# Pooled attention and a GELU MLP on one core: the loads of the fourth group placed behind the transposes of the softmax weights

## The chip, the cores and the metric

The kernel runs on one core of a Trainium2 chip. The metric is device time in microseconds (us), taken as the median of several runs. The kernel before took 294.56 us (three runs, 293.27 to 294.96). The profiled execution of it has a span of 291.9 us. All times inside the kernel are counted from the start of that span.

## What is computed

Eight batches of attention come first. Keys and values are averaged over blocks of eight rows, so that 576 queries meet 72 pooled keys. Then every token passes an MLP with a tanh GELU. Shapes: q, k and v are 8 x 8 heads x 576 x 64, in float32; the MLP goes from 512 to 2048 and back to 512, for 4608 tokens.

```python
k_p = k.reshape(B, H, Sp, pool, D).mean(axis=3)        # pool = 8, Sp = 72
v_p = v.reshape(B, H, Sp, pool, D).mean(axis=3)
scores = scale * np.matmul(q, k_p.transpose(0, 1, 3, 2))
attn = np.exp(scores - scores.max(-1, keepdims=True))
attn = attn / (attn.sum(-1, keepdims=True) + 1e-09)
x = np.matmul(attn, v_p)                               # then heads side by side: 4608 x 512
h = x @ w_in
g = 0.5 * h * (1.0 + np.tanh(c * (h + 0.044715 * h * h * h)))
out = g @ w_out
```

## The kernel before

The tokens are taken in nine groups. Groups 0 to 7 are the first 512 queries of each batch; the remainder R holds the last 64 queries of all eight batches. The order is 0, 1, ..., 6, R, 7, and **step n** is the MLP of the n-th group in it. The kernel is a software pipeline. While step n runs its MLP on TensorE, the attention of the next group (n+1) is worked out in between, and the inputs of the group after that (n+2) are loaded. So step 1 runs the MLP of group 1, the attention of group 2 and the loads of group 3.

Instructions are placed by hand. `at(hooks, slot, f, ...)` says ahead of which matmul of the step's MLP a piece of other work is put into the programs of its engines. Slots 0 to 63 lie in the first half of the MLP (64 matmuls with w_in, "hidden"), slots 64 to 175 in the second (seven products of 16 matmuls each). A slot fixes the order of the instructions on each engine, not a time: an instruction starts when it is at the head of its engine's program and what it waits for has come.

All DMAs are issued by SyncE, one after the other: loads, stores, and the three kinds of transposes that the DMA engines do. `kTd` is the transposed pooled K, `qT` the transposed queries, `eT` the transposed softmax weights, in four parts j = 0 to 3.

```python
if kv:
    t0 = 22 if n_ == 1 else 12
    at(hooks, t0, pool, b, 0, 5)             # VectorE: sums K (and the first half block of V) over 8 rows
    at(hooks, t0, dup_k, b, 0, 5)
    at(hooks, t0, kT_tile, b, None)
    at(hooks, t0, k_transpose_dma, b)        # SyncE: kTd
    t1 = t0 + (16 if n_ == 1 else 24)
    at(hooks, t1, pool, b, 5, 9)             # VectorE: the rest of V
    at(hooks, t1, spread_v, b, nc.gpsimd)
    at(hooks, 56, k_spread, b, [nc.vector, nc.vector])
for j in range(4):
    sj = 64 + ([4, 4, 30, 34] if n == R else [4, 7, 28, 36])[j]
    at(hooks, sj, scores, n, j)              # TensorE
    at(hooks, sj, exps, n, j)                # ScalarE
    ...
    nj = 64 + [17, 33, 40, 50][j]
    at(hooks, nj, norm, n, j, nc.gpsimd if j == 1 else nc.vector)   # writes eb
    at(hooks, nj, e_transpose_dma, n, j)     # SyncE: eT, part j
...
at(hooks, 64 + 92, values_part, n, 0, [nc.scalar, nc.vector])       # TensorE: needs eT parts 0 and 1
...
if n_ > 1:
    at(hooks, 4, values_part, g, 1, [nc.scalar, nc.vector])         # parts 2 and 3, in the next step
```

`pool` sums blocks c0 to c1 of one tile that holds K and V. Blocks 0 to 3 are K; block 4 is half K and half V; blocks 5 to 8 are V. So `pool(b, 0, 5)` waits for three loads, and `pool(b, 5, 9)` for the fourth:

```python
def load_kv(n):
    if n != B - 1:
        b = B - 1 if n == R else n
        kv_tile(b)
        load_main(b, "k", 0, 4, nc.sync)     # 1 MB
        load_half(b, "k", nc.sync)           # 128 KB
        load_half(b, "v", nc.sync)           # 128 KB
        load_main(b, "v", 0, 4, nc.sync)     # 1 MB
```

In the second half of the MLP, the sums of activations (`g_sums`, VectorE) and the copy of the first product out of its PSUM bank (`x_copy`, VectorE) come ahead of the product called 6, which reads the sums and writes that bank again:

```python
for n, (prod, acc, fresh) in enumerate([(1, xs, 1), (2, y, 1), (6, xs, 0), (5, z, 1), (7, xs, 0), (3, z, 0), (4, xs, 0)]):
    ...  # 16 matmuls of product `prod` into bank `acc`
    if prod == 1:
        x_copy(nc.vector, k2)
```

After the norms, `cast_gated` (GpSimd) turns the queries of the group after the next into bf16, and `q_transpose_dma` transposes them at slot 164, for the scores of the next step.

Of the kernel before, what the change touches and what calls it, by code (L numbers as in the profile page):

```python
# [19 lines left out]
def kernel(  # L20
# [21 lines left out]
    nc = tc.nc  # L42
# [10 lines left out]
    R = B  # L53
# [622 lines left out]
    def at(hooks, s, f, *a):  # L676
        hooks.setdefault(s, []).append(lambda: f(*a))
# [6 lines left out]
    hooks = {}  # L684
# [42 lines left out]
    for n_, g in enumerate(seq):  # L727
        if n_ == 0:
            continue
        hooks = {}  # L730
        if n_ == 1:
            for i in range(1, 4):
                at(hooks, i, w_sums, i, 0, NP, nc.vector)
            at(hooks, 36, g_sums, 0, 4)
        else:
            at(hooks, 20, g_sums, 0, 2)
            at(hooks, 36, g_sums, 2, 4)
        at(hooks, 57, g_sums, 4, 6)
        at(hooks, 65, g_sums, 6, 8)
        if n_ + 1 < len(seq):  # L740
            n = seq[n_ + 1]
            b = B - 1 if n == R else n
            kv = n != B - 1
            if n_ == 1:
                for j in range(4):
                    at(hooks, 28 + 4 * j, cast_q, n, j, j + 1, nc.scalar)
                at(hooks, 41, qT_tile, n)
                at(hooks, 41, q_transpose_dma, n)
            if kv:
                t0 = 22 if n_ == 1 else 12  # L750
                at(hooks, t0, pool, b, 0, 5)
                at(hooks, t0, dup_k, b, 0, 5)
                at(hooks, t0, kT_tile, b, None)
                at(hooks, t0, k_transpose_dma, b)
                t1 = t0 + (16 if n_ == 1 else 24)
                at(hooks, t1, pool, b, 5, 9)
# [4 lines that stand above are left out]
                at(hooks, sj, scores, n, j)  # L761
                at(hooks, sj, exps, n, j)
                if j == 0:
                    at(hooks, 64 + 17, eT_tile, n)
                nj = 64 + [17, 33, 40, 50][j]
                at(hooks, nj, norm, n, j, nc.gpsimd if j == 1 else nc.vector)
                at(hooks, nj, e_transpose_dma, n, j)
            at(hooks, 64 + 66, nc.scalar.preload_act_table_set, GELU_SET)
            at(hooks, 64 + 92, xT_tile, n)
            at(hooks, 64 + 92, values_part, n, 0, [nc.scalar, nc.vector])  # L770
        if n_ > 1:
            at(hooks, 4, values_part, g, 1, [nc.scalar, nc.vector])
        if n_ + 2 < len(seq):
            n2 = seq[n_ + 2]
            if n2 != R:
                at(hooks, 57, q_tile, n2)
                at(hooks, 57, load_q, n2, 0, 4, nc.sync)
            at(hooks, 64 + 52, cast_gated, n2)
            at(hooks, 64 + 100, qT_tile, n2)
            at(hooks, 64 + 100, q_transpose_dma, n2)  # L780
            at(hooks, 44 if n_ == 1 else 28, load_kv, n2)
        if n_ == 1:
            at(hooks, 58, q_tile, R)
        if 1 <= n_ <= 4:
            at(hooks, 58, load_q, R, n_ - 1, n_, nc.sync)
        mlp(g, hooks, n_ + 1 == len(seq), n_ > 1)


# [28 lines left out]
```

The softmax here doesn't subtract the row's maximum and nothing guards it: scores larger than these inputs give would overflow.

## Time and profile before

The page of the profile lists each engine's busy time as a share of the span.

| | busy us | share of the span |
|---|---|---|
| TensorE matmuls (PE) | 277.1 | 95% |
| TensorE weight loads (PEld), beside them | 198.2 | 68% |
| VectorE (DVE) | 206.7 | 71% |
| ScalarE (ACT) | 166.8 | 57% |
| GpSimd (POOL) | 63.7 | 22% |
| DMA queue of SyncE, share of 16 engines | | 71.9% |

A matmul counts as busy from start to end, so the busy share says little on its own; the idle stretches, and what ends them, say more. The profile cuts the span into 40 slices of 7.3 us each, and gives each engine's busy share in tenths for each slice, with the clock that TensorE was granted. The waits name, for an engine, the instruction that sat idle and what released it. In the DMA queue's timeline a start is when SyncE began to issue the transfer, the duration is the issuing, and the time to landing is counted from the start.

### The profile page before, as it was taken

To read this page: it belongs to the slowest core of one execution; us is meant where nothing else is said; L and a number is where in the kernel's file an instruction comes from. 1 tells how busy PE (TensorE), PEld (TensorE's weight loads), DVE (VectorE), ACT (ScalarE), POOL (GpSimd) and SP (SyncE) were. 2 spreads that over 40 slices of the span, in tenths; PEclk is the share of its full clock that TensorE was granted. 3 is DMA by queue.
4 is the path that set the end of the run, shared out by engine and by line. 5 is a ranking of instruction groups with operands and counts; after the bars stand their busy time and mean duration, and the time that the engine had idled before them with its cause. 6 is when DMAs were issued, how large, how long until landed. Compare 5 with 4: busy or idle time off the path is not lost.

```text
span 291.9 us, 5584 instructions
## 1 busy us (share of the span) xinstructions
PE 277.1 (95%) x2193; PEld 198.2 (68%) x2203; DVE 206.7 (71%) x379; ACT 166.8 (57%) x262; POOL 63.7 (22%) x97
## 2 busy tenths in 40 slices
PE   7799999999669999999999999999999999999994
PEld 3578753447547498649865986598658965985583
DVE  5891879899617896789588958994899445944531
ACT  1586574786306663666467547754675467546510
POOL 4575343012120312031203120312031200100000
PEclk9999999999979999999999999999999999999999
DMA  7999999999948894899779957915731560144003
GB/s 232 353 386 342 378 384 189 324 273 268 279 89 219 268 261 94 217 266 261 111 196 315 213 124 186 310 37 137 184 129 36 130 144 2 37 99 101 1 2 145
DMA packets 71419, 56.41 MB, mean 193 GB/s; under 512 B 45664, under 2 KB 55392, under 8 KB 71392
## 3 DMA queue, kind: packets, MB, share of 16 engines
q1 hardware_dynamic: 71392, 56.04, 71.9%
q8 instruction: 17, 0.28, 0.4%
q14 instruction: 10, 0.08, 0.1%
HBM read 36.70 MB, written 9.44 MB: 158 GB/s over the span
## 4 chain that ended last, share of the span: by engine, by line
PE 79%; DMA 11%; SPq 4%; DVE 4%; issue 1%; POOL 0%
PE mm L485 31%; PE mm L380 28%; PE mm L391 8%; DMA w_out_s<-in_moe_w_out_dram 5%; PE xo L348 4%; DMA stage<-in_moe_w_in_dram 3%; PE x L485 2%; PE sc L229 2%; SPq L555 2%; DMA eT<-eb 1%; DMA qT<-q_b 1%; DVE eb L263 1%; PE mm L396 1%; DVE den L251 1%; SPq L108 1%
## 5 line engine op out<-in xcount | busy, mean ns | idle before, releaser
L380 PE MATMUL mm<-xT,w_in_b 128*128 128x512 bf16 x392 | 87.4, 379 | 0.4
L382 ACT ACTIVATE gT<-mm 128x512 bf16<-128x512 f32 x100 | 59.6, 598 | 24.9 <-PE mm L380 24.9
L380 PEld LDWEIGHTS <-w_in_b 128*128 128x128 bf16 x400 | 39.1, 98 | 45.8 <-issue 0.3
L485 PEld LDWEIGHTS <-gT 128*128 128x128 bf16 x512 | 49.4, 98 | 7.3
L169 POOL TENSOR_TENSOR vbd<-kvb,vmask 128x256 bf16<-128x256 bf16 (+2 forms) x40 | 23.6, 613 | 97.4 <-DVE kvb L149 97.3
L391 PE MATMUL mm<-xT,w_in_b 128*128 128x256 bf16 x352 | 42.2, 273 | 0.2 <-DVE xT L90 0.2
L485 PEld LDWEIGHTS <-stage 128*128 128x128 bf16 x384 | 37.4, 98 | 4.4
L391 PEld LDWEIGHTS <-w_in_b 128*128 128x128 bf16 x352 | 34.0, 98 | 4.2 <-issue 0.3
L90 DVE CAST xT<-xo 128x512 bf16<-128x512 f32 x16 | 11.1, 691 | 34.5 <-PE xo L348 29.7
L393 ACT ACTIVATE gT<-mm 128x512 bf16<-128x512 f32 x44 | 26.2, 597 | 15.4 <-PE mm L391 15.4
L485 PE MATMUL mm<-w_out_b,gT 128*128 128x256 bf16 x240 | 30.8, 273 | 0.0
L244 ACT ACTIVATE e<-sc 128x576 f32<-128x576 f32 x36 | 22.5, 650 | 11.5 <-PE sc L229 6.9
L485 PE MATMUL mm<-tw,gT 128*128 128x256 bf16 x240 | 28.8, 273 | 0.0
L88 ACT COPY osb<-mm 128x512 f32<-128x512 f32 x23 | 13.5, 587 | 26.7 <-PE mm L485 26.0
L251 DVE TENSOR_REDUCE den<-e 128x8 f32<-128x576 f32 x36 | 26.4, 734 | 2.3 <-ACT e L244 2.3
L485 PE MATMUL mm<-tw,stage 128*128 128x256 bf16 x224 | 27.9, 273 | 0.0
L147 DVE TENSOR_TENSOR kv<-kv 128x1024 f32<-128x1024 f32 (+3 forms) x19 | 21.0, 1107 | 7.9 <-DMA kv<-in_k_dram 6.1
L431 DVE TENSOR_TENSOR stage<-gT 128x512 bf16<-128x512 bf16 (+1 forms) x31 | 16.4, 528 | 12.7 <-ACT gT L382 7.4
L88 ACT CAST xT<-xo 128x512 bf16<-128x512 f32 (+1 forms) x18 | 11.3, 634 | 24.2 <-PE xo L348 16.8
L263 DVE TENSOR_TENSOR eb<-e,r 128x576 bf16<-128x576 f32 x24 | 20.4, 848 | 0.8
L432 DVE TENSOR_TENSOR gT<-gT 128x512 bf16<-128x512 bf16 (+1 forms) x31 | 14.8, 477 | 6.4 <-ACT gT L382 4.8
L263 POOL TENSOR_TENSOR eb<-e,r 128x576 bf16<-128x576 f32 x6 | 6.9, 1151 | 52.6 <-ACT e L244 46.7
(86 smaller groups left out, 301.7 us busy)
## 6 DMA issues: line engine op xcount, KB each, us to landing
kv<-in_k_dram SPq DMA_DIRECT2D x7, 1024.0 KB, 6.8
q_sb<-in_q_dram SPq DMA_DIRECT2D x7, 1024.0 KB, 11.7
out_dram<-osb SPq DMA_DIRECT2D x13, 512.0 KB, 3.0
kv<-in_v_dram SPq DMA_DIRECT2D x6, 1024.0 KB, 8.8
kv<-in_v_dram SPq DMA_DIRECT2D x4, 512.0 KB, 10.2
w_in_s<-in_moe_w_in_dram SPq DMA_DIRECT2D x4, 512.0 KB, 9.0
stage<-in_moe_w_in_dram SPq DMA_DIRECT2D x4, 512.0 KB, 11.5
w_out_s<-in_moe_w_out_dram SPq DMA_DIRECT2D x2, 1024.0 KB, 13.3
```

The lines of the kernel that those rows point to most:

```text
L88: eng.copy(out=out, in_=in_)
L147: add(out=t[:, :, 0:4, :], in0=t[:, :, 0:4, :], in1=t[:, :, 4:8, :], op=ALU.add)
L169: eng.tensor_tensor(out=vbd[p0:128, b, n0:n1, :].rearrange("p (c r) (hh d) -> p c (r hh) d", c=max(m, 1), d=D), in0=kvb[p0:128, 4 + c0:4 + ...
L244: nc.scalar.activation(out=e.rearrange("p (x h) s -> p x (h s)", x=2), in_=sc[:, :, 0:4 * Sp], func=ACT.Exp, scale=1.0 / 64.0)
L251: nc.vector.reduce_sum(out=den, in_=e, axis=AX.X)
L263: eng.tensor_tensor(out=o.rearrange("p (h s) -> p h s", s=Sp), in0=e, in1=r.unsqueeze(2).to_broadcast([128, H, Sp]), op=ALU.mult)
L380: nc.tensor.matmul(out=hp, lhsT=w_in_b[:, ko, fo * 128:(fo + 1) * 128], rhs=st[g]["xT"][:, ko, :], start=(i == 0), stop=(i == KO - 1))
L382: nc.scalar.activation(out=gT[:, fo, :], in_=hp, func=ACT.Gelu_apprx_tanh)
L391: nc.tensor.matmul(out=hp[:, f, :], lhsT=w_in_b[:, ko, (fo + f) * 128:(fo + f + 1) * 128], rhs=st[g]["xT"][:, ko, c0:c0 + 256], start=(ko ...
L393: nc.scalar.activation(out=gT[:, fo:fo + 2, c0:c0 + 256], in_=hp, func=ACT.Gelu_apprx_tanh)
L431: nc.vector.tensor_tensor(out=s3, in0=a11, in1=a21, op=ALU.subtract)
L485: nc.tensor.matmul(out=xs[p] if acc is xs else acc[:, p, :], lhsT=lt, rhs=rt, start=bool(fresh and m == 0 and (p == 0 or (last and acc is ...
```

## The change

The change moves DMA issues of SyncE, and nothing else. In the kernel before, step 1 issues at slot 44 the loads of K and V of group 3 (2.25 MB), at slots 57 and 58 the queries of group 3 (1 MB) and a part of the remainder's queries (two transfers of 128 KB, each of 512 short rows), and only then the four transposes eT of group 2. After it, step 1 issues at slot 44 only the queries of group 3, then the four transposes, then at slot 116 K and V of group 3. The four parts of the remainder's queries are loaded in steps 2 to 5 instead of 1 to 4. In step 2 the slots of the pooling are moved back, from 12 and 36 to 18 and 42.

Its purpose is that the transposes of the softmax weights of group 2 need not queue behind 3.5 MB of loads in step 1. Data, sizes and arithmetic stay the same, and so do the numbers of instructions on every engine.

```diff
@@ -747,7 +747,7 @@
             if kv:
-                t0 = 22 if n_ == 1 else 12
+                t0 = {1: 22, 2: 18}.get(n_, 12)
                 at(hooks, t0, pool, b, 0, 5)
                 at(hooks, t0, dup_k, b, 0, 5)
                 at(hooks, t0, kT_tile, b, None)
@@ -773,16 +773,17 @@
         if n_ + 2 < len(seq):
             n2 = seq[n_ + 2]
             if n2 != R:
-                at(hooks, 57, q_tile, n2)
-                at(hooks, 57, load_q, n2, 0, 4, nc.sync)
+                s2 = 44 if n_ == 1 else 57
+                at(hooks, s2, q_tile, n2)
+                at(hooks, s2, load_q, n2, 0, 4, nc.sync)
             at(hooks, 64 + 52, cast_gated, n2)
             at(hooks, 64 + 100, qT_tile, n2)
             at(hooks, 64 + 100, q_transpose_dma, n2)
-            at(hooks, 44 if n_ == 1 else 28, load_kv, n2)
+            at(hooks, 64 + 52 if n_ == 1 else 28, load_kv, n2)
         if n_ == 1:
             at(hooks, 58, q_tile, R)
-        if 1 <= n_ <= 4:
-            at(hooks, 58, load_q, R, n_ - 1, n_, nc.sync)
+        if 2 <= n_ <= 5:
+            at(hooks, 58, load_q, R, n_ - 2, n_ - 1, nc.sync)
```

## The prediction

> **What bounds the kernel now.** I read the slices first, to find where TensorE is not full; then TensorE's waits, to name what ended the gap; then busy time by step, to see what the gap costs; then the DMA queue's timeline, for the cause.
>
> ```profile
> PE   7799999999669999999999999999999999999994
> ...
> PEclk9999999999979999999999999999999999999999
> ```
>
> Each digit is 7.3 us. TensorE is full everywhere but in the first two slices, the last, and slices 11 and 12 (73 to 88 us). In the second of these the granted clock drops as well. The longest wait of TensorE stands there alone:
>
> ```profile
> PE xo L348 <- DMA eT<-eb: 5.0, 1, 5.0
> ```
>
> The columns are total us, times, longest us. L348 are the matmuls of values_part, and what they waited for is a transposed part of the softmax weights. The timeline of TensorE dates it:
>
> ```profile
> 76.50 1.47 PE L485 MATMUL mm<-w_out_b,stage 128*128 128x256 bf16 x12
> 82.99 1.86 PE L348 MATMUL xo<-eT,vbd 128*128 128x256 bf16 x8 [5.01 <-DMA eT<-eb]
> ```
>
> I took a step as running from its first matmul with w_in to that of the next, and asked for busy times of those stretches (the length comes first, then PE, PEld, DVE, ACT and POOL, the clock, the DMA share):
>
> ```profile
> 52.36:87.54 35.18, 29.67 (x201) 19.52 (x201) 25.26 (x40) 18.79 (x31) 6.32 (x9) 0.95 1.02 242
> 87.54:116.36 28.82, 28.77 (x225) 21.34 (x225) 23.20 (x42) 17.55 (x27) 6.18 (x9) 1.00 0.87 209
> 116.36:145.19 28.83, 28.78 (x226) 21.35 (x225) 23.20 (x42) 17.55 (x27) 6.18 (x9) 1.00 0.89 212
> ```
>
> Steps 2 and 3 are full of matmuls: TensorE bounds them, with 0.05 us idle. Step 1 is 6.36 us longer, though it has eight values matmuls (0.87 us) fewer, so it has about 7.2 us to give. The DMA queue's timeline says why:
>
> ```profile
> 65.41 0.59 SPq L108 DMA_DIRECT2D kv<-in_k_dram  x1
> 66.05 0.53 SPq L103 DMA_DIRECT2D kv<-in_k_dram  x1
> 66.62 0.60 SPq L101 DMA_DIRECT2D kv<-in_v_dram  x1
> 67.27 0.59 SPq L108 DMA_DIRECT2D kv<-in_v_dram  x1
> 67.90 0.62 SPq L120 DMA_DIRECT2D q_sb<-in_q_dram  x1
> 68.56 5.16 SPq L124 DMA_DIRECT2D q_r<-in_q_dram  x2
> 73.83 8.94 SPq L293 DMA_TRANSPOSE eT<-eb  x4
> ```
>
> Part 0 of the weights was ready at 72.37 us (end of its norm on VectorE), but SyncE was issuing the remainder's queries until 73.7. Once issued, part 0 took 8.0 us to land and part 1 4.4 us (issued 78.49, landed 82.9); in step 3 the same transposes take 2.6 to 2.9. The wait in step 1 is thus for 3.5 MB ahead in the queue: the last remainder load, issued 71.9, landed 9.3 us later, at 81.2, and the transposes right after it.
>
> **What the Trainium skill says.** The page "DMA: Bandwidth & Descriptors", section "Queues, rings and completion order", says that on each DMA engine the descriptors of a queue are consumed in ring order. This trace agrees: transposes ready before 75 us land just behind the loads issued before them, at 81.8 and 82.9. The same page, "Issuing engines are not separate DMA queues", says that all issuers share the same 16 engines; no run so far shows it, but it tells me that order is the only thing to gain here. The page "TensorE: Matmul & The Clock Gate", section "What's actually happening", says that an idle window of about 3.4 us halves the clock. The trace agrees: after 5.01 us idle the granted clock in 82 to 86 us is 0.56 to 0.58 and the first values matmuls take 417 ns instead of 273.
>
> **The change, part by part.**
>
> (a) The removed wait. TensorE reaches the values matmuls at 76.50 + 1.47 = 77.97. After the change only 1 MB of queries lies ahead of the transposes, issued at 65.4; at the 340 GB/s that the stretches 68 to 78 show, it is in by about 71. Part 1 is normed on GpSimd until 74.55; plus 2.6 to land is 77.2. So the wait vanishes with 0.8 us to spare: 5.0 us off.
>
> (b) The slow clock after it. From the first values matmul to the next step took 87.54 - 82.99 = 4.55 us here, 116.36 - 113.31 = 3.05 in step 2. That is another 1.5 us. Sum of (a) and (b): **6.5 us**. Step 2 would start at 77.97 + 3.05 = 81.0 instead of 87.54.
>
> (c) The moved loads. K and V of group 3 are now issued behind part 3, which is normed at 76.9 and issued from about 77.0 to 78.2. So K starts at 78.3. From the issue of K to the landing of the V half, the third transfer that the first pooling needs, it took 6.9, 8.2, 7.0 and 7.9 us in steps 2 to 5. It will land at 85.2 to 86.5, say 85.8. When would VectorE want it?
>
> ```profile
> 89.32 0.69 DVE L90 CAST xT<-xo 128x512 bf16<-128x512 f32 x1 [2.88 <-PE xo L348]
> 89.93 1.48 DVE L147 TENSOR_TENSOR kv<-kv 128x1280 f32<-128x1280 f32 x1
> ...
> 95.16 0.42 DVE L431 TENSOR_TENSOR stage<-gT 128x512 bf16<-128x512 bf16 x1 [0.16 <-ACT gT L382]
> 96.02 0.43 DVE L432 TENSOR_TENSOR gT<-gT 128x512 bf16<-128x512 bf16 x1 [0.44 <-ACT gT L382]
> ```
>
> These are VectorE's in step 2: pooling begins 2.4 us into the step, so it would want K at 81.0 + 2.4 = 83.4, **2.4 us before it is there**. Moving the pooling from slot 12 to 18 doesn't help: no other VectorE work lies between these slots, and its order of instructions is the same in both kernels. VectorE then has 0.16 + 0.44 us of waits to swallow, and none more until its last osb sum 25 us into the step: it runs about 1.8 us late through the middle of step 2.
>
> (d) What that lateness costs. Two things hang on it. First, product 6 must wait for x_copy: this ended at 105.43, and product 6 began at 106.34, so 0.9 us are free, and 1.8 late costs 0.9. Second, the transposes: pooling releases kTd, and behind it SyncE issues K and V of group 4, its queries and the remainder's, all 2.4 us later. In step 2 of before the last of these landed at 100.5 + 10.5 = 111.0, and parts 0 and 1 behind it at 111.8 and 112.6, while TensorE came for them at 113.31: 0.7 us free. Shifted by 1.8 to 2.4 us, TensorE is held 1.1 to 1.7 us in all; the 0.9 at product 6 is contained in that, not added. I take **1.5 us**. Two short waits don't reach the 3.4 us at which the clock falls.
>
> (e) The remainder's queries move from steps 1 to 4 to steps 2 to 5. Steps 2 to 4 keep one part each. Step 5 has no queries of a next group to load, so it has room; GpSimd casts them only at 198.3 us, some 11 us after that slot (slot 58 lies 58 hidden matmuls of 0.22 us and 0.9 us of values into a step that begins at 174.0). I charge nothing.
>
> Sum: 294.56 - 6.5 + 1.5 = 289.6; I round to 289.5.
>
> **The rivals.** *Full recovery*: K lands in time, or VectorE's lag is swallowed, and 6.5 us come off: 288.1. For it: K would start on a queue that holds only two transposes. Against it: K was issued on an almost empty queue in steps 2 to 5 as well and still needed 6.9 us. *A wait handed on*: step 2 becomes what step 1 was. The transposes of the queries of group 3 come behind K and V, SyncE is held in issuing them, kTd and the loads of group 4 slip 3 us or more, and TensorE waits 3 to 4 us, perhaps with the slow clock again: 291 to 293. For it: eT part 0 took 4.56 us to issue into a full queue instead of 1.2. Against it: kTd has until about 2 us ahead of the scores, and the pooling, not the queue, should end last. *Another bound at the old place*: part 1 comes from GpSimd; if it lands 1 us later than I reckon, 0.2 us of the gain go, not more.
>
> **Range and chances.** The gain is 6.5 less a hand-back between 0 and 3.5 us, most likely 1 to 2; medians of before scatter over 1.7 us. So 288.0 to 291.2 holds it 8 times in 10. Faster by over 2% means under 288.67, which needs a hand-back of 0.6 or less: 0.27. Slower by over 2% has no mechanism: 0.01.
>
> **What would show it.** Right: no wait of L348 near 78 us, no clock drop there, step 1 about 28.7 us; in step 2 a wait of VectorE's pooling (L147) for kv of about 2.4 us, and TensorE waits of 1 to 2 us at product 6 (L485, for the copy) or at L348 (for eT); step 3 again 28.8. Wrong: step 2 at 28.8 (K came in time), or at 31 and more with a clock below 1.00 (the wait was handed on), or a wait of over 0.5 us still at the first values matmuls of step 1.

## The result, and the profile after

The changed kernel takes 290.52 us (median of four runs, 289.53 to 290.72) against 294.48 us before: a ratio of 0.9869, with a 95% interval from 0.9838 to 0.9899. That is 4.0 us less. The prediction said 289.5, within 288.0 to 291.2, with a gain most likely under 2%.

The slices of the profile after, again 40 with 7.2 us each; the rows of the other engines are left out:

```profile
PE   8778999999999988999999999999999999999994
...
PEclk9999999999999999999999999999999999999999
```

The two 6s at 73 to 88 us are gone, and the clock no longer falls. Two 8s have come at 101 to 115 us, which is step 2. TensorE's waits (total us, times, longest us) name what stands there:

```profile
PE xo L348 <- DMA eT<-eb: 1.1, 1, 1.1
...
PE mm L485 <- DVE osb L90: 0.9, 1, 0.9
...
PE sc L229 <- DVE kbd L90: 0.4, 1, 0.4
```

The busy times by step, with the steps cut as before (length, then PE, PEld, DVE, ACT, POOL, clock, DMA share, GB/s), for steps 1, 2 and 3:

```profile
53.12:81.66 28.54, 28.16 (x201) 18.95 (x201) 25.04 (x40) 18.73 (x31) 6.21 (x9) 1.00 0.83 204
81.66:113.37 31.71, 29.26 (x226) 21.31 (x225) 23.21 (x42) 17.43 (x27) 6.17 (x9) 1.00 1.05 260
113.37:142.19 28.82, 28.77 (x226) 21.31 (x225) 23.20 (x42) 17.54 (x27) 6.17 (x9) 1.00 0.90 212
```

This is the whole account. Step 1 went from 35.18 to 28.54 us: **6.64 us won**. Step 2 went from 28.82 to 31.71: **2.89 us given back**. From step 3 on nothing moved. The net is 3.75 us, close to the 4.0 of the medians; the start-up was 0.76 us longer in this one profile (step 1 begins at 53.12, not 52.36), so the two spans differ by only 3.1.

The give-back begins in SyncE's DMA timeline (start, duration of the issuing):

```profile
72.93 5.99 SPq L293 DMA_TRANSPOSE eT<-eb  x4
78.98 0.57 SPq L108 DMA_DIRECT2D kv<-in_k_dram  x1
79.60 0.51 SPq L103 DMA_DIRECT2D kv<-in_k_dram  x1
80.15 0.59 SPq L101 DMA_DIRECT2D kv<-in_v_dram  x1
80.79 0.59 SPq L108 DMA_DIRECT2D kv<-in_v_dram  x1
...
82.21 8.70 SPq L220 DMA_TRANSPOSE qT<-q_b  x1
...
92.05 1.23 SPq L199 DMA_TRANSPOSE kTd<-kvb  x1
93.33 0.57 SPq L108 DMA_DIRECT2D kv<-in_k_dram  x1
```

The four transposes now land 2.6 us after each issue, as predicted. K starts at 79, and VectorE stands waiting for the third of these loads, the half block of V:

```profile
83.46 0.69 DVE L90 CAST xT<-xo 128x512 bf16<-128x512 f32 x1 [2.64 <-PE xo L348]
87.13 1.49 DVE L147 TENSOR_TENSOR kv<-kv 128x1280 f32<-128x1280 f32 x1 [2.99 <-DMA kv<-in_v_dram]
```

And TensorE pays for it at three places of step 2, with its idle time in brackets:

```profile
97.22 0.41 PE L229 MATMUL sc<-kbd,qT 128*128 128x144 bf16 x4 [0.38 <-DVE kbd L90]
...
102.11 0.60 PE L485 MATMUL mm<-tw,stage 128*128 128x256 bf16 x4 [0.93 <-DVE osb L90]
...
110.16 1.03 PE L348 MATMUL xo<-eT,vbd 128*128 128x256 bf16 x8 [1.08 <-DMA eT<-eb]
```

The three waits are 2.39 us; the remaining 0.5 us is matmuls that overlap less where TensorE has to start again (29.26 us busy against 28.77 in step 3).

### The profile page after: what moved, and what is told of

Same layout as the page of the kernel before. It is cut to its first block, busy times and chain, and to the rows that moved or that the text cites. A ratio compares the mean times of both kernels' runs of the same rounds, so it can differ in the third digit from the quotient of the medians.

```text
span 288.8 us, 5583 instructions
## 1 busy us (share of the span) xinstructions
PE 276.6 (96%) x2193; PEld 197.7 (68%) x2203; DVE 207.7 (72%) x379; ACT 166.5 (58%) x262; POOL 62.4 (22%) x97
## 3 DMA queue, kind: packets, MB, share of 16 engines
q1 hardware_dynamic: 71392, 56.04, 72.3%
## 4 chain that ended last, share of the span: by engine, by line
PE 78%; DVE 9%; DMA 8%; SPq 2%; issue 1%; POOL 1%; ACT 0%; DVEq 0%; ACTq 0%
PE mm L485 27%; PE mm L380 25%; PE mm L391 11%; PE mm L396 5%; PE xo L348 3%; DMA q_sb<-in_q_dram 3%; PE x L485 2%; DMA kv<-in_v_dram 2%; PE sc L229 2%; DMA qT<-q_b 1%; DMA eT<-eb 1%; DVE eb L263 1%; DVE kv L147 1%; SPq L108 1%; DVE w_in_b L90 1%
## 5 line engine op out<-in xcount | busy, mean ns | idle before, releaser
L90 DVE CAST xT<-xo 128x512 bf16<-128x512 f32 x16 | 11.1, 691 | 28.6 <-PE xo L348 23.7
```

## The experiments

The theory to test: eT waited in step 1 for the loads ahead of it; and of step 2's waits, the first two come from VectorE, late because the half block of V came late, the third from the DMA queue. Each run is compared with the kernel before on the same chip.

### Is it the late half block of V that costs in step 2? (K early)

```diff
 # the change, but:
-            at(hooks, 64 + 52 if n_ == 1 else 28, load_kv, n2)
+            if n_ == 1:
+                at(hooks, 44, ...)        # K and the two half blocks, 1.25 MB, right behind the queries
+                at(hooks, 64 + 52, load_main, n2, "v", 0, 4, nc.sync)
+            else:
+                at(hooks, 28, load_kv, n2)
```

> The change, but with K of group 3 and the two half blocks (1.25 MB) issued ahead of the transposes right behind the queries; only the last 1 MB of V goes behind. My theory: the first pooling of step 2 then waits for nothing, VectorE isn't late, and all three waits of TensorE in step 2 (0.38, 0.93, 1.08 us) go; 2.25 MB ahead of the transposes are in by about 74, so the wait of step 1 stays away: 288.1 us. Rival: it is the queue, not VectorE, that costs in step 2 (the queries' transposes of group 3 hold SyncE 8.7 us behind V); then the wait for eT of 1.1 us stays and this is about 289.3. Second rival: 2.25 MB ahead are too much, eT part 1 lands after 78.5, and a wait of 0.5 us or more returns in step 1.

Measured: 287.64 us, ratio 0.9762 (0.9733 to 0.9791), so clearly below the change itself. TensorE's waits from 50 us to the end, all of them:

```profile
PE xo L348 <- DMA eT<-eb: 0.5, 1, 0.5
PE sc L229 <- DMA qT<-q_b: 0.4, 1, 0.4
```

The first is in step 1 (at 78.8 us), the second was there in the kernel before as well. All three waits of step 2 are gone, and so is VectorE's for V: step 2 is 28.8 us. The second rival is right too: with 2.25 MB ahead, part 1 landed at 78.7, and 0.53 us of wait came back in step 1. It is the fastest version of this study.

### Is the third wait of step 2 the queue or VectorE? (no remainder in step 2)

```diff
-        if 2 <= n_ <= 5:
-            at(hooks, 58, load_q, R, n_ - 2, n_ - 1, nc.sync)
+        if 3 <= n_ <= 5:
+            at(hooks, 58, load_q, R, n_ - 3, n_ - 2 if n_ < 5 else 4, nc.sync)
```

> The change, but with none of the remainder's queries in step 2 (one part in steps 3 and 4, two in step 5). If the last wait of step 2 (1.08 us for eT) is the queue behind late loads, it goes, while the 0.38 for kbd and the 0.93 at product 6, which are VectorE's lateness, stay: 289.4 us. If that wait is VectorE's lateness as well (the norm of part 1 itself too late), all stays: 290.5 us. Two parts in step 5 should cost nothing, since no queries of a next group are loaded there; if they do, a wait shows in step 5.

Measured: 288.70 us, ratio 0.9808 (0.9771 to 0.9844). TensorE's waits after 50 us:

```profile
PE sc L229 <- DVE kbd L90: 0.7, 1, 0.7
PE mm L485 <- DVE osb L90: 0.6, 1, 0.6
PE sc L229 <- DMA qT<-q_b: 0.4, 1, 0.4
```

The wait for eT is gone; the two on VectorE stay and sum to 1.3 us, as with the whole change. So the third wait was the queue, filled to the end by 256 KB of short rows. Step 2 takes 30.45 us here, 1.63 more than in the kernel before: that is what VectorE's lateness costs alone. The two parts in step 5 show no wait. The time is 0.7 us lower than I expected.

### Does SyncE, held while it issues, cause the third wait? (V behind the queries' transposes)

```diff
 # the change, but K and the half blocks at slot 116, and
+                at(hooks, 64 + 101, load_main, n2, "v", 0, 4, nc.sync)     # behind q_transpose_dma at 164
```

> The whole change, but the last 1 MB of V of group 3 is issued behind the transposes of the queries of group 3, not ahead of them. K and the half blocks stay late. My theory: VectorE is as late as before (pooling waits 3 us), so the waits for kbd and at product 6 stay (1.3 us in sum); but SyncE is no longer held 8.7 us in issuing the queries' transposes, kTd goes out when K is pooled, the loads of group 4 start 1.7 us earlier, and the wait for eT in step 2 (1.08 us) falls to 0.3 or less: 289.6 us. Rival: being held is harmless and the eT wait comes from VectorE's lateness alone: 290.5 us.

Measured: 291.82 us, ratio 0.9896 (0.9861 to 0.9931): no faster than the whole change. My theory fell. TensorE in step 2, then the second pooling of VectorE:

```profile
97.92 0.41 PE L229 MATMUL sc<-kbd,qT 128*128 128x144 bf16 x4 [1.43 <-DVE kbd L90]
...
102.82 0.60 PE L485 MATMUL mm<-tw,stage 128*128 128x256 bf16 x4 [0.93 <-DVE osb L90]
...
111.05 1.03 PE L348 MATMUL xo<-eT,vbd 128*128 128x256 bf16 x8 [1.27 <-DMA eT<-eb]
```

```profile
94.61 1.23 DVE L147 TENSOR_TENSOR kv<-kv 128x1024 f32<-128x1024 f32 x1 [0.80 <-DMA kv<-in_v_dram]
```

K of group 4 did go out earlier (91.87 instead of 93.33), but the last remainder load behind it landed later (109.7 instead of 108.7). That SyncE is held (6.8 us here, 8.7 with the change) looks like a sign of a full queue, not a cause of its own: with 2.25 MB moved into step 2, what counts is when all the bytes are through. The DMA share of step 2, 1.05 after and 0.87 before, says the same. The run is not a clean test, since it also made V later (the 0.80 us), and that added to the wait for kbd.

### What does each part of the change do alone?

The remainder's queries alone, on the kernel before:

```diff
-        if 1 <= n_ <= 4:
-            at(hooks, 58, load_q, R, n_ - 1, n_, nc.sync)
+        if 2 <= n_ <= 5:
+            at(hooks, 58, load_q, R, n_ - 2, n_ - 1, nc.sync)
```

> The kernel before with one part of the change alone: the remainder's queries from step 2 on; K and V of group 3 stay ahead of the transposes. My theory: the short rows of the remainder's queries were the last thing in the queue. Without them K, V and queries (3.4 MB at 340 GB/s from 67 us) are in by about 77 to 78, eT part 1 lands at about 79, TensorE waits about 1 us instead of 5.0, its clock stays at 1.00, and step 2 isn't late: 289 to 290 us. Rival: the 2.25 MB of K and V are what holds the transposes, and the 256 KB are worth their bytes, 0.75 us: the wait is still over 4 us, the clock still falls, 293.5 to 294.

K, V and the queries of group 3 alone, which is the whole change with that edit undone:

```diff
-        if 2 <= n_ <= 5:
-            at(hooks, 58, load_q, R, n_ - 2, n_ - 1, nc.sync)
+        if 1 <= n_ <= 4:
+            at(hooks, 58, load_q, R, n_ - 1, n_, nc.sync)
```

> The other part of the change alone: K and V of group 3 behind the transposes and its queries ahead, but the remainder's queries where they were (steps 1 to 4). Ahead of the transposes lie 1 MB of queries and 256 KB of short rows. My theory: that is in by about 75, part 1 lands at 77.5 to 78.5, the wait of step 1 is 0.5 us at most, and step 2 is as late as with the whole change: 290.5 to 291. So the two parts don't add up: either alone takes most of the gain. Rival: the short rows are what matters, a wait of 2 us or more stays in step 1, 292.5.

Measured: 291.25 us for the remainder alone (0.9887, 0.9843 to 0.9931), 291.43 us for K and V alone (0.9877, 0.9820 to 0.9933). Each wins some 3.4 us, and both together 4.0, so they don't add up. The remainder's part leaves this wait in step 1, in a profile of the fastest of its four runs (290.20 us):

```profile
80.91 1.03 PE L348 MATMUL xo<-eT,vbd 128*128 128x256 bf16 x8 [2.67 <-DMA eT<-eb]
```

It is 2.67 us, where I had expected 1 and the rival over 4: the queries landed at 79.6, not by 78. Still, 256 KB were worth 2.3 us, three times their 0.75 us by bytes, since their short rows move slowly: in the kernel before, 158 GB/s came through from 78 to 79 us, when nearly all packets were of 256 B, against 340. The still lower rates in the next two us (113 and 22 GB/s) are not theirs: without them the stretch behind the queries is as slow, 58 GB/s from 78 to 79 us. Step 2 gives nothing back. The K and V part leaves no wait in step 1, and this one in step 2, which I had expected as with the whole change:

```profile
110.64 1.76 PE L348 MATMUL xo<-eT,vbd 128*128 128x256 bf16 x8 [2.55 <-DMA eT<-eb]
```

Its last remainder load landed at 109.4 and part 1 at 110.6. Counted from the start of step 2, part 1 is 0.9 us later than with the whole change. Why, when the same bytes were ahead in that step, stays open. Its four runs spread over 3.3 us (289.5 to 292.8) and the profile is of the slowest, so this wait need not be the same each time.

### Do the slots of the pooling matter?

```diff
-                t0 = {1: 22, 2: 18}.get(n_, 12)
+                t0 = 22 if n_ == 1 else 12
```

> The change with the pooling of step 2 back in slots 12 and 36. My theory: the slot only fixes the order on VectorE, and no other work of VectorE lies between the old and the new slots, so nothing moves: 290.5 us as with the whole change, within 0.5. Rival: the later slot is what keeps VectorE from being held early in step 2; then this is 0.5 to 1 us slower, and the wait of the pooling for V (2.99 us) grows.

Measured: 290.89 us, ratio 0.9867 (0.9835 to 0.9898). The same as the whole change, within the scatter; VectorE's wait for V is 2.99 us there and 3.02 here, and the instructions of VectorE, GpSimd and SyncE stand in the same order in both traces. This line of the change does nothing. Step 2 is 32.43 us in this profile and 31.71 in that of the whole change, so single profiles differ by 0.7 us in this step with the order unchanged.

### Is the slow clock a cost of its own?

The kernel before, with TensorE kept busy in its wait. The 20 matmuls on zeros are no part of the reference:

```diff
+            if n_ == 1:
+                at(hooks, 64 + 92, warm_up, 20, "sc")
             at(hooks, 64 + 92, xT_tile, n)
```

> The kernel before, with 20 matmuls on zeros (0.22 us each, 4.3 us in all) put into TensorE's program just ahead of the values matmuls of step 1, where it waits 5.0 us. They do no work of the reference. The wait for eT is as long, but TensorE is idle only 0.7 us of it. My theory: the clock then stays at 1.00 and the 1.5 us after the wait are saved: 293.1 us against 294.6. Rival: the slow stretch comes from something else (the transposes' traffic), then the clock still falls and the time is as before.

Measured: 293.20 us, ratio 0.9947 (0.9930 to 0.9965), which is 1.6 us less (1.0 to 2.1) for 20 matmuls more.

```profile
77.85 4.48 PE L591 MATMUL warm<-zeros 128*128 128x512 bf16 x20
82.95 1.03 PE L348 MATMUL xo<-eT,vbd 128*128 128x256 bf16 x8 [0.62 <-DMA eT<-eb]
```

The values matmuls begin at 82.95, as in the kernel before (82.99), but take 1.03 us instead of 1.86. The 1.5 us of the slow clock were a separate term, and idleness was its cause.

### Is it the order in one queue, or the traffic?

I had said that a transpose waits because descriptors of a queue are taken in order. So I gave the loads another queue. First, on the kernel with only the remainder moved, K, V and queries of group 3 from GpSimd:

```diff
-                at(hooks, 57, load_q, n2, 0, 4, nc.sync)
+                at(hooks, 57, load_q, n2, 0, 4, nc.gpsimd if n_ == 1 else nc.sync)
-            at(hooks, 44 if n_ == 1 else 28, load_kv, n2)
+            at(hooks, 44 if n_ == 1 else 28, load_kv, n2, nc.gpsimd if n_ == 1 else nc.sync)
```

> The kernel with only the remainder's queries moved (wait for eT in step 1: 2.67 us), but K, V and the queries of group 3 (3.25 MB) are issued by GpSimd in step 1 instead of SyncE, at the same slots; the transposes stay with SyncE. GpSimd is free for them from about 67.5 us, 2.5 us later than SyncE, so the loads end at about 80 to 82. Theory: a transpose waits because it stands behind the loads in SyncE's own queue. Then from a queue of its own it passes them: part 1 lands by 79, the wait is 1 us or less. Rival: it waits because the 16 DMA engines are busy with 3.25 MB, whatever the queue; then it lands behind them at 81 to 82 and the wait is 3 us or more, with the slow clock. In time 288 to 289.5 against 292 to 293; step 2 may give back up to 1 us, since the queries land and are cast later.

Then on the whole change, K and V alone, back at slot 44 and issued by GpSimd:

```diff
-            at(hooks, 64 + 52 if n_ == 1 else 28, load_kv, n2)
+            at(hooks, 44 if n_ == 1 else 28, load_kv, n2, nc.gpsimd if n_ == 1 else nc.sync)
```

> The whole change, but K and V of group 3 go back to slot 44 of step 1 and are issued by GpSimd (2.25 MB), its queries ahead of the transposes by SyncE. If a queue of its own lets the transposes pass, the wait of step 1 is 0.5 us or less, K is there long before step 2 wants it, and step 2 has no waits: 287.5 us, as good as K early. If the engines' traffic is what counts, part 1 lands at 79 or later, a wait of 1 us or more: 288.5 or more.

Measured: 294.39 us (0.9992, 0.9975 to 1.0010) and 291.58 us (0.9887, 0.9833 to 0.9941). From the first: GpSimd's last load, SyncE's transposes, and TensorE's wait:

```profile
70.19 0.92 POOL L120 DMA_DIRECT2D q_sb<-in_q_dram  x1
```

```profile
72.33 8.92 SPq L293 DMA_TRANSPOSE eT<-eb  x4
```

```profile
82.46 1.86 PE L348 MATMUL xo<-eT,vbd 128*128 128x256 bf16 x8 [4.44 <-DMA eT<-eb]
```

The queries took 11.1 us and landed at 81.2. Part 0 of eT, alone in SyncE's queue and issued at 72.3, landed 9.3 us later, at 81.6; part 1 at 82.3. In the second kernel V landed at 79.7, part 0 at 80.8, and the wait was 2.89 us. So the rival is right: loads under way hold the transposes up, whichever queue they come from. The first kernel's packets from 77 to 79.5 us say how (packets, MB, share of the 16 engines; q0 is there only when GpSimd issues):

```profile
q0 software_dynamic: 206, 0.82, 93.7%
q1 hardware_dynamic: 206, 0.05, 11.1%
```

The transposes were not kept back until the loads were done. The engines moved as many packets of SyncE's queue as of GpSimd's, but the transposes' packets are of some 256 B and the loads' of some 4 KB, so the transposes got about a sixteenth of the bytes. From 72.3 to 76.5 us no packet of SyncE's queue moved at all; why is not shown. The Trainium skill says on the page "DMA: Bandwidth & Descriptors", section "Issuing engines are not separate DMA queues", that the DMAs of all issuers run on the same 16 engines and interleave. No run had shown it when I cited the page; this trace agrees.

### One try at more

```diff
 # K early, without the remainder in step 2, and the queries of group 3 behind the transposes
-                s2 = 44 if n_ == 1 else 57
+                s2 = 64 + 51 if n_ == 1 else 57
```

> A try at more than with K early: only K and the half blocks (1.25 MB) ahead of the transposes, the queries of group 3 and then the last of V behind them, and the remainder's queries from step 3 on. Ahead lie 1 MB less than with K early, so the 0.53 us of wait in step 1 should go; but the queries land at about 83, their cast and transposes end later, SyncE is held and kTd of step 2 may slip. If kTd slips by less than 2 us: 287.1 us. If it slips by more, waits for kbd or qT of 0.5 to 2 us come in step 2: 288 to 289.5.

Measured: 288.96 us, ratio 0.9798 (0.9760 to 0.9835). The wait of step 1 is gone, and these two came in step 2, where I had expected waits for kbd or qT:

```profile
PE xo L348 <- DMA eT<-eb: 0.7, 1, 0.7
PE mm L485 <- DVE osb L90: 0.4, 1, 0.4
```

The queries' transposes went out at 88.2 and kTd at 92.1, against 81.7 and 87.6 with K early. Late queries cost more than the 0.5 us they could save.

## Why the prediction was right, and where it was off

The gain was right to 0.14 us. What step 2 gives back was nearly twice what I reckoned, and the number still lies in the range because that left room for up to 3.5 us of it.

**(a) The wait**: right. TensorE reached the first values matmuls at 77.14 + 1.47 = 78.61, or 77.85 with the 0.76 us of slower start taken off, against 77.97 predicted. Part 1 had landed 0.9 us before, against 0.8 predicted.

**(b) The slow clock**: right, 1.5 us as worked out from the trace and 1.6 measured by itself with the warm wait. Parts (a) and (b) together were 6.5 and came out at 6.64.

**(c) The late K**: the mechanism was right, and its size short. VectorE began to pool 87.13 - 81.66 = 5.5 us into step 2, not 4.8, so it was 3.1 us late instead of 2.4. K went out when predicted; the V half needed 8.1 us from there, not 7.5.

**(d) What the lateness costs** is the term that was mis-sized: 1.5 us said, 2.89 measured. Both of its parts were short.

- *VectorE.* Its x_copy was 2.5 us late (19.72 us into the step instead of 17.21), not 1.8. Less the 0.9 us that were free, this makes 1.6, as the run without the remainder in step 2 shows alone (1.63). A part of it fell at kbd, where I had seen no cost.
- *The transposes*, which end last. I shifted them by 1.8 to 2.4 us, on the reckoning that the loads of group 4 move by the 2.4 us of the pooling. These loads went out 11.67 us into the step instead of 6.84. That is 4.8 us later: 3.1 by the pooling, and 1.7 more because SyncE was issuing the queries' transposes behind K and V for 8.70 us. The last of them landed 3.6 us later than before, and part 1 of eT 3.3 us later. How much of this is the later issue, and how much the 2.25 MB more in the step, no run separates cleanly; the one with V behind the queries' transposes speaks for the bytes. Less the 0.7 us that were free, and with what TensorE needs to start again, this makes the 2.89.

That VectorE's waits are contained in the hold by the transposes, and not added to it, fits these sums. The rival of a wait handed on was nearer than I thought: it named SyncE's being held and a slip of 3 us or more, and step 2 did come to over 31 us. But TensorE waited 2.39 us and not 3 to 4, and the clock stayed full.

**(e) The remainder**: right that steps 3 to 5 pay nothing.

**The slots**: right that they do nothing.

**The clock as a limit**: the statement that short waits don't reach the 3.4 us was right for the change, and isn't safe: with K and V alone the clock was 0.50 in 112 to 114 us, after an idle time of 2.55 us (and one of 0.83 us some 7 us before it).

**The reason given for (a)**, order within a queue, was too narrow: from another queue the loads hold the transposes up just as well, so they must not be under way at that time.

## What to carry to other kernels

When a small urgent transfer sits behind bulk loads, moving the bulk behind it only pays as far as whoever waits for the bulk has time to spare; so look up the next consumer's slack first, and split the bulk there (here K, wanted 2.4 us into the next step, ahead, and V, wanted 10 us into it, behind: 287.6 instead of 290.5 us). Putting the bulk on another engine's queue was no way round here: both queues share the DMA engines, and the transposes, in small packets, got few of the bytes beside the loads in large ones. And price a long wait of TensorE at more than its length, since the clock that falls with it costs on.

## What the hardware showed that I had not expected

- The clock fell after TensorE had been idle for 5.01, 4.44, 2.89 and 2.55 us, but not after 2.67 us in the profiled run of the remainder alone. The Trainium skill's page "TensorE: Matmul & The Clock Gate", section "What's actually happening", gives a window of about 3.4 us; these runs show that less can be enough. The other runs of the remainder alone had mean clocks of 0.992 to 0.993 and took 290.7 to 292.7 us, against 290.2 at full clock. That they lost the clock after this very wait is likely, but no profile of them is shown.
- The transposes that the DMA engines do for SyncE landed no sooner than loads of GpSimd's queue that had been issued 2 to 5 us earlier: 9.3 us to land instead of 2.6, with as many packets moved as the loads from 77 to 79.5 us, but a sixteenth of their bytes.
- Where loads end and transposes follow, there is a stretch in which hardly anything moves: 22 GB/s from 80 to 81 us in the kernel before, 58 from 78 to 79 with the remainder alone moved, 7 from 108 to 109 with K and V alone. So a transpose behind loads waits for more than their bytes. Why is not shown.
- The transposes of the queries, 3.2 us to issue in the kernel before, took 8.7 us behind 2.25 MB and held everything that SyncE had to issue after them.
